# Attention and gated GELU block on one core: the pass over a unit's maxima set ahead of the V product, four bias additions and four closing additions dealt anew

## Chip, cores and metric

One core of one Trainium2 chip runs the whole program. The metric is the device time of one execution in microseconds. The time of a kernel is the median of several executions; a profile comes from one execution of its own, whose time is given beside its span.

## What is computed

The input x has 2048 tokens of 512 values. Its layer norm goes into two branches: attention with 32 heads of 16 values, and a dense block with a tanh-approximated GELU of 1376 hidden values, whose output goes through SiLU and gates the attention's output. x is added at the end.

```python
qkv = (xn @ wqkv).reshape(B, S, 3, H, Dh)           # xn = layernorm(x)
scores = einsum("bhqd,bhkd->bhqk", q, k) * Dh ** -0.5
s = einsum("bhqk,bhkd->bhqd", softmax(scores), v).reshape(B, S, D) @ wo
g = silu(gelu(xn @ w1 + b1) @ w2 + b2)
out = x + s * g
```

All matrices are f32. Most products are made of three: each factor is split into a high part (ScalarE's copy to the fp32r type) and a low part (the rest), and high x high, high x low and low x high are summed.

## The kernel before

**Work and its order.** The program's schedule is written out by hand; nothing is reordered. Each engine has one queue and works through it in order. The pools only give addresses. The program has three stages.

*Stage A* (to about 478 us): layer norm, the projections to Q, K and V, and the dense block. `down` multiplies hidden values by w2; the sums of four token tiles of 128 rows stand in four PSUM banks (`PA[c]`, one of `ps_v`, three of `ps_t`) and are taken out when a chunk `c` of 512 tokens is done (L649 to L661). For the first three chunks ScalarE copies the four tiles to SBUF (L656) and each becomes a `chore`: GpSimd adds the bias b2 (L666) and issues the store to `g_d` (L667); `half` calls one chore at a time. For the last chunk VectorE adds the bias straight from PSUM (L654), four times, and GpSimd issues the four stores (L661).

*The loop* (about 480 to 1545 us) works on 32 units: unit `u` is four heads and 512 queries. It has 513 steps, 16 for each unit. In a step, four score products with the keys in the partitions (`t_one`, letter T, L737) are each followed by an exponential on ScalarE (L739), and one V product (`pv_step`, letter V, L800) takes the exponentials of the step before. The exponential needs each query's largest score, which must be known ahead. So the loop also computes the scores of later units with the queries in the partitions (L190) and takes their maxima on VectorE (`s_max`, L195). A whole tile of these is letter S. Letters X and Y are two halves of one such tile, on the two row halves of TensorE, in one bank: Y must wait until X is finished, and this goes through a token, an instruction without work on GpSimd (in `s_op`, L227): it waits for X, and Y waits for it. The order of a step is a string, mostly `TSXTTSTYV`: three maxima a step. From step 50 on one step in 16 (that with two steps behind the end of a unit's V product) has `TSTTSTV`, two maxima.

**The end of a unit's maxima.** A unit has 64 maxima, and it reaches them in the middle of the loop's steps: 22 units (9 to 30) end in the part that matters here, the last (31) near step 491. `done` counts them, and at 64 the unit goes to `ended`. `s_end0` then takes one more pass over the unit's maxima on VectorE (`nm`, L250: 16 values for each partition out of 128), puts the split of `nm` into two parts on GpSimd into `put_off` (L253, L254, run behind the next token), has the queries of unit `u + 2` loaded, and puts the unit into `later` with a count (12 in stage A, 8 in the loop). Each V counts it down by 4; at zero `s_end1` transposes on VectorE (L269) and stores to `mh_d` through SP; `load_mh` reads it back for the score products.

Which maximum calls `s_end0` is decided in `s_max`, and there lies the first edit:

```python
done[u] += 1
if ended:
    s_end0(ended.pop())
if done[u] == 64:
    ended.append(u)
```

So `nm` stands one maximum behind the unit's last one: within the next step if that was a step's third, and at the same step's end if it was the second.

**Other lines used below.** At the last step of a unit's V product VectorE copies the bank `pv` to `os` (L807), which frees it for the next unit; `o_den` takes a reciprocal (L828), `o_div` a product (L837, GpSimd, for the last unit VectorE). Key loads of later heads are issued by GpSimd within the steps (L110).

*The end* (from 1545 us): the output projection (L81, L906) of the tokens that are left, the last four tiles (12 to 15) together. `w_gate` multiplies the product by the gate (L916), `w_add` adds x (L921) and stores through SP (L922). Tile 15 goes in two halves.

Of the kernel before, what the change touches and what calls it, by code (L numbers as in the profile page):

```python
# [16 lines left out]
P = 128  # L17
# [4 lines left out]
KT = D // P  # L22
NT = S // P
CH = 512
NCH = S // CH
# [24 lines left out]
def fused(ctx: ExitStack, tc: tile.TileContext, x, wqk, wv, wo, w1, b1, w2, b2, out):  # L50
    nc = tc.nc
# [92 lines left out]
    def load_qs(u, sides=range(2)):  # L144
        if u < NU:
            QS[u] = qzs[u % 2] if u < LEAD // 16 else qss[0][:, u % 2]
            q_rows(QS[u], u, sides)

    def ask_qs(u):
        errands[:0] = [(load_qs, u, (a,)) for a in range(2)]  # L150
# [13 lines left out]
    later, ended, errands, sent = [], [], [], set()  # L164

    def tick():
        for e in later:
            e[0] -= 1

    def flush():  # L170
        while later and later[0][0] <= 0:
            u = later.pop(0)[1]
            run_off()
            s_end1(u)

    def at_of(job):
        u, st, p = job
        return divmod(st, NCH) if u else divmod(st, NCH)[::-1]
# [13 lines left out]
    def s_max(ps, job, heads, parts):  # L192
        u, p = job[0], job[2]
        qi, ki = at_of(job)
        nc.vector.tensor_reduce(MX[u][:, 2 * p:2 * p + 2, qi, ki][:, heads, parts], ps.rearrange("p (n c) -> p n c", c=HC), axis=AX.X, op=OP.max)  # L195
        done[u] += 1
        if ended:
            s_end0(ended.pop())
        if done[u] == 64:
            ended.append(u)  # L200
        if done[NU - 1] == 64:
            s_end0(ended.pop())

    def s_whole(job, a):
        ps = s_tile()[0]
        s_mm(ps, job, a, 0, 0, CH)
        s_max(ps, job, a, slice(0, 2))
# [33 lines left out]
    def run_off():  # L241
        while put_off:
            put_off.pop(0)()

    def s_end0(u):
        later.append([12 if "seen" in prog else 8, u])
        nm = qring.tile([P, GH * NCH], F32, name="nm")
        hl = NM[u] = qring.tile([P, 2, GH * NCH], F32R, name="nmh")
        mx = MX.pop(u).rearrange("p a b c n -> p (a b) (c n)")
        nc.vector.tensor_reduce(nm, mx, axis=AX.X, op=OP.max, negate=True)  # L250

        def two():
            nc.gpsimd.tensor_copy(hl[:, 0], nm)  # L253
            nc.gpsimd.tensor_sub(hl[:, 1], nm, hl[:, 0].bitcast(F32))  # L254

        put_off.append(two)
        if "seen" in prog or u == NU - 1:
            run_off()
        del QS[u]
        if "seen" in prog:  # L260
            ask_qs(u + 2)
        else:
            load_qs(u + 2)

    prog = {}
# [14 lines left out]
    b2_sb = xp.tile([P, D], F32, name="b2_sb")  # L280
# [17 lines left out]
    for i in range(nu):  # L298
        pairs.append(ms[2 * i:2 * i + 2])
        if (i + 1) * len(qs) // nu > i * len(qs) // nu:  # L300
            g, c = qs[i * len(qs) // nu]
# [4 lines left out]
    for j in range(len(pairs)):  # L306
        for h in range(2):
# [9 lines left out]
            n = 2 if nd < len(parts) and parts[nd][2] and ready - nd > room else 1  # L317
            n = max(n, need - 2 * (left - 1))
            while nd < ready and n > 0:
                c, f, k = parts[nd]  # L320
# [25 lines left out]
    def w2_load(i):  # L346
        if i < len(ms):
            W2[ms[i][1:]] = w_new(w2[ms[i][2]], 2, "raw2")

    def w2_split(i):  # L350
        if i < len(ms):
            W2[ms[i][1:]] = w_split(W2[ms[i][1:]], "w2", W2B)
# [31 lines left out]
    with ExitStack() as s1:  # L384
# [14 lines left out]
        def load_x(t):  # L399
            xs[t] = w1k.tile([P, D], F32, name="xt", bufs=XB)  # L400
            eng = nc.scalar if t in (1, 3) else nc.sync
            eng.dma_start(xs[t], x[t * P:(t + 1) * P, :])
# [57 lines left out]
            W1[g] = w_new(wqk[:, g], 2, "raw1")  # L460
        for t in range(4, 6):
            load_x(t)
        for k in range(KT):
            nc.sync.dma_start(wv_r[:, k], wv[:, k])
        for t in range(6, XB):
            load_x(t)
# [112 lines left out]
    def mark(dve=False):  # L579
        if dve:  # L580
            i = nc.vector.tensor_copy(junk[:, 1:], ident_r[:1, :1].bitcast(F32)).ins
        else:
            i = nc.scalar.activation(junk[:, :1], ident_r[:1, :1].bitcast(F32), AF.Copy).ins  # L583
        tc.add_manual_dep(i, latest[0][1], SYNC, reason="row tile done")
        tokens.append((latest[0][0], i.name))

    def mark_early(n):
        if prog["seen"] < n:
            mark()
# [3 lines left out]
    def run(ops, hooks={}):  # L593
        for n, two in enumerate(zip(*ops)):
            prog["n"] += 1
            for a in range(2):
                fill(a)
                mm(a, *two[a])
            for h in hooks.get(n, []):
                h()  # L600
# [23 lines left out]
    PA, chores = {}, []  # L624

    def down(c, f, part):
        i = c * FT + f
        if f == 0 and part == 0:
            PA[c] = [ps_v.tile([P, D], F32, name="pv")] + [ps_t.tile([P, D], F32, name="pst") for t in range(3)]
        h, w = HS[c, f], W2[c, f]  # L630
        side = (part + i) % 2
        ops = [[], []]
        for a in range(2):
            for t in ((0, 1), (2, 3))[(a + side) % 2]:
                ts = slice(t * P, (t + 1) * P)
                for n, (x, y) in enumerate(((0, 0), (0, 1), (1, 0))):
                    ops[a].append(((c, t), PA[c][t], h[x][:, ts], w[y],
                                   f == 0 and part == 0 and n == 0, f == FT - 1 and part == 1 and n == 2))
        n = prog["pe"]
        if (c, f, part) == parts[-2]:  # L640
            run(ops, {2: [lambda: mark(True)], 5: [lambda: mark(True)]})
        else:
            run(ops, {3: [lambda: mark_early(n)]})
        if part == 0:
            w2_split(i + 1)
            w2_load(i + 3)
            return
        del HS[c, f], W2[c, f]
        if f == FT - 1:  # L649
            both = [wk.tile([P, 2, CH], F32R, name="gt") for i in range(2)]  # L650
            for n, t in enumerate((0, 2, 1, 3)):
                gt = both[n // 2][:, n % 2].bitcast(F32)
                if c == NCH - 1:
                    nc.vector.tensor_add(gt, PA[c][t], b2_sb)  # L654
                else:
                    nc.scalar.activation(gt, PA[c][t], AF.Copy)  # L656
                rs = slice(c * CH + t * P, c * CH + (t + 1) * P)
                if c < NCH - 1:
                    chores.append((gt, rs))
                else:  # L660
                    nc.gpsimd.dma_start(g_d[rs, :], gt)  # L661

    def chore():
        if chores:
            gt, rs = chores.pop(0)
            nc.gpsimd.tensor_add(gt, gt, b2_sb)  # L666
            nc.gpsimd.dma_start(g_d[rs, :], gt)  # L667

    def errand():
        if errands:  # L670
            f, *args = errands.pop(0)
            f(*args)
# [92 lines left out]
            load_mh(0)  # L765
    while errands:
        errand()
    del prog["seen"]
    s_ring.append(ps_x)
    qz.close()  # L770
# [108 lines left out]
    def cols(t):  # L879
        n = 2 if t == NT - 1 else 1  # L880
        return [slice(i * D // n, (i + 1) * D // n) for i in range(n)]
# [32 lines left out]
    def w_gate(t, i=0):  # L914
        gx, cs = GX[t], cols(t)[i]
        nc.vector.scalar_tensor_tensor(gx[:, 0, cs], PW[t][i][:, :cs.stop - cs.start], 0.5, gx[:, 0, cs],  # L916
                                       op0=OP.mult, op1=OP.mult)

    def w_add(t, eng, i=0):
        gx, cs = GX[t], cols(t)[i]  # L920
        eng.tensor_add(gx[:, 0, cs], gx[:, 0, cs], gx[:, 1, cs])  # L921
        nc.sync.dma_start(out[t * P:(t + 1) * P, cs], gx[:, 0, cs])  # L922

    def w_out(t, eng):
        w_gate(t)
        w_add(t, eng)
# [9 lines left out]
    def due(n):  # L936
        return min(4 * L, 4 * LEAD + max(0, 3 * n - 1 - max(0, (n - LIGHT) // 16)))

    for u in range(NU):
        g, c = divmod(u, NCH)  # L940
# [13 lines left out]
    T3 = range(NT - NCH, NT)  # L954
    late = range(NW, NT)
    for t in range(0, NW, 2):
        n = DONE + 2 * t
# [9 lines left out]
    for i, t in enumerate(late):  # L967
        n = L - 2 * len(late) - 1 + 2 * i
# [9 lines left out]
    for n in range(L + 1):  # L978
        ua, ka = divmod(n, 16)
        want = due(n) - due(n - 1)  # L980
        i = 0
        for op in ORDER[want] if n > 1 else ("TTTTV", "TVTSTST")[n]:
            if op in "SXY":
                s_op(op)
            elif op == "V":
                if n:
                    pv_step(*divmod(n - 1, 16))
                for _ in range(4):
                    tick()
                flush()  # L990
            else:
                if EARLY <= 4 * n + i < 4 * L:
                    t_one(ua, ka, i % 2, 1 - i // 2)
                for f, args in todo.get((n, i), []):
                    f(*args)
                i += 1
# [15 lines left out]
    for n, (t, i) in enumerate(ends):  # L1012
        w_mul(t, KS[-2:], (i,))
        w_gate(t, i)
        w_add(t, nc.vector if n else nc.gpsimd, i)


# [31 lines left out]
```

## Time and profile before

| what | value |
| --- | --- |
| median of 3 runs | 1568.05 us (1567.88 to 1568.91) |
| profiled execution | 1567.75 us |
| its span | 1566.0 us |
| granted TensorE clock | 1.00 |
| TensorE, VectorE, ScalarE, GpSimd busy | 99%, 89%, 79%, 24% of the span |
| from 490 to 1470 us: VectorE, ScalarE busy | 912.93 and 976.75 of 980 us |

In the profile PE is TensorE's products, PEld its loads of weights, DVE is VectorE, ACT ScalarE, POOL GpSimd and SP the queue of DMAs; a q behind a name is that engine's sequencer. A row of a timeline has the start and the duration in us, the engine, the line, the operation, out<-in with shapes, the count, and in brackets the idle time of the engine before it with what ended it. A row of the waits has the waiting engine, tile and line, who ended the wait, and total us, times and the longest. A row of the windows gives the stretch, then busy us and instructions of PE, PEld, DVE, ACT and POOL, the clock and the DMA share. Matmuls are pipelined, so TensorE's busy time holds waiting as well. Two instructions of one engine can overlap in their rows by some 0.1 us.

### The profile page before, as it was taken

Reading aid. Unit: us, or ns where it says so; the run is one execution under the profiler, and the core shown is the slowest. Engines: PE = TensorE matmul, PEld = TensorE weight load, DVE = VectorE, ACT = ScalarE, POOL = GpSimd, SP = SyncE. Lnnn points to the kernel's source line nnn. Section 1 sums busy time; section 2 is a strip of 40 time slices with the busy share of each in tenths; the row PEclk is TensorE's granted clock in tenths of the full one; section 3 lists DMA queues with packets and bytes.
Section 4 is the critical chain, followed back from the end, with each engine's and each line's share of the span. In section 5 each row is a group of like instructions: output and inputs, shape, how many; then the busy total and the mean of one; then the engine's idle time right before and its main releaser. Section 6 shows DMA issues by size and latency. Waiting matters only on the chain.

```text
span 1566.0 us, 32580 instructions
## 1 busy us (share of the span) xinstructions
PE 1555.4 (99%) x12254; PEld 955.0 (61%) x12254; DVE 1390.1 (89%) x2306; ACT 1244.4 (79%) x2487; POOL 375.4 (24%) x392
## 2 busy tenths in 40 slices
PE   8999999999999999999999999999999999999998
PEld 7899999999995444444444444444444444444455
DVE  7899999999998999999999999999999999999833
ACT  4333343434338999999999999999999999999994
POOL 4135574756752000000000100010110000000144
PEclk9999999999999999999999999999999999999999
DMA  6515443356435012311111311131141111110162
GB/s 217 159 47 139 116 156 108 112 148 152 140 89 117 21 42 43 60 30 30 43 29 28 65 30 43 43 73 36 36 73 30 33 29 30 43 30 22 45 209 104
DMA packets 79501, 117.38 MB, mean 75 GB/s; under 512 B 28876, under 2 KB 29132, under 8 KB 77968
## 3 DMA queue, kind: packets, MB, share of 16 engines
q1 hardware_dynamic: 75884, 102.36, 23.8%
q0 software_dynamic: 2976, 12.35, 4.4%
q8 instruction: 97, 1.59, 0.4%
q10 hardware_dynamic: 484, 0.60, 0.1%
q14 instruction: 60, 0.49, 0.1%
HBM read 84.81 MB, written 25.97 MB: 71 GB/s over the span
## 4 chain that ended last, share of the span: by engine, by line
PE 98%; DVE 1%; DMA 0%; issue 0%; POOL 0%; ACT 0%; DVEq 0%
PE pv L800 33%; PE pst L737 15%; PE ps L737 14%; PE ps L569 13%; PE ps L190 10%; PE pst L569 7%; PE pv L569 3%; PE ps L906 2%; PE ps L450 1%; PE ps L81 1%; PE pst L81 1%; DVE st L411 0%; DMA xt<-in_x 0%; PE pst L434 0%; DVE slot L76 0%; DVE xn L425 0%
## 5 line engine op out<-in xcount | busy, mean ns | idle before, releaser
L195 DVE TENSOR_REDUCE mx<-ps 128x2 f32<-128x512 f32 x2048 | 1297.3, 684 | 109.2 <-PE ps L190 29.1
L739 ACT ACTIVATE slot<-pst 128x512 f32<-128x512 f32 x1533 | 803.6, 604 | 2.9 <-PE ps L190 1.6
L800 PE MATMUL pv<-slot,vsb 128*17 128x512 f32 (+1 forms) x4096 | 539.2, 598 | 0.1
L190 PE MATMUL ps<-kt,slot 48*128 48x512 f32 x1350 | 382.7, 371 | 1.1 <-POOLq L227 1.1
L739 ACT ACTIVATE slot<-ps 128x512 f32<-128x512 f32 x515 | 307.9, 598 | 7.5 <-PE ps L737 4.7
L737 PE MATMUL pst<-qt,kt 50*128 50x512 f32 x1149 | 304.4, 405 | 0.0
L737 PEld LDWEIGHTS ps<-qt,kt 50*128 50x128 f32 x387 | 70.7, 183 | 323.8 <-ACT slot L739 322.9
L190 PEld LDWEIGHTS ps<-kt,slot 48*128 48x128 f32 x1350 | 223.1, 184 | 5.4 <-POOLq L227 1.4
L569 PE MATMUL ps<-slot,w1h 64*128 64x512 f32 x1104 | 222.3, 393 | 0.0
L737 PEld LDWEIGHTS pst<-qt,kt 50*128 50x128 f32 x1149 | 207.4, 184 | 21.3 <-DVE gt L654 1.2
L737 PE MATMUL ps<-qt,kt 50*128 50x512 f32 x387 | 190.9, 495 | 0.0
L190 PE MATMUL ps<-kt,qz 48*128 48x512 f32 x448 | 186.8, 417 | 0.0
L190 PE MATMUL ps<-slot,slot 48*128 48x512 f32 x584 | 168.5, 372 | 0.0
L569 PEld LDWEIGHTS ps<-slot,w1h 64*128 64x128 f32 x1104 | 156.0, 185 | 5.0 <-ACT junk L583 0.2
L569 PE MATMUL ps<-slot,w1l 64*128 64x512 f32 x552 | 145.3, 392 | 0.0
L370 POOL TENSOR_TENSOR hl<-hg,hh 128x512 fp32r<-128x512 f32 x76 | 96.9, 1297 | 134.6 <-ACT hh L369 94.4
L800 PEld LDWEIGHTS pv<-slot,vsb 128*17 128x17 f32 (+1 forms) x4096 | 68.8, 96 | 83.7 <-issue 31.6
L583 ACT ACTIVATE junk<-ident_r 1x1 f32<-1x1 f32 x94 | 18.4, 196 | 126.3 <-PE pst L569 118.2
L737 PE MATMUL pst<-qt,slot 50*128 50x512 f32 x384 | 99.6, 405 | 0.0
L190 PEld LDWEIGHTS ps<-slot,slot 48*128 48x128 f32 x584 | 97.1, 184 | 3.3 <-DVE mx L195 1.2
L837 POOL TENSOR_TENSOR slot<-slot,dn 64x512 f32<-64x512 f32 x16 | 20.5, 1281 | 312.4 <-PE pst L737 167.3
L190 PEld LDWEIGHTS ps<-kt,qz 48*128 48x128 f32 x448 | 82.0, 183 | 15.4 <-DVE mx L195 0.8
(153 smaller groups left out, 1764.2 us busy)
## 6 DMA issues: line engine op xcount, KB each, us to landing
raw<-in_w SPq DMA_DIRECT2D x88, 256.0 KB
qk_h<-hh SPq DMA_DIRECT2D x32, 256.0 KB
qk_l<-hl SPq DMA_DIRECT2D x32, 256.0 KB
qt<-qk_h SPq DMA_DIRECT2D x128, 64.0 KB
slot<-qk_h SPq DMA_DIRECT2D x92, 64.0 KB
g_d<-gt POOLq DMA_DIRECT2D x16, 256.0 KB, 3.0
qt<-qk_l SPq DMA_DIRECT2D x64, 64.0 KB
kt<-qk_h POOLq DMA_DIRECT2D x16, 256.0 KB, 6.4
```

The source lines that it names most:

```text
L81: nc.tensor.matmul(ps, lhs[a], rhs[b], start=first and n == 0, stop=last and n == 2)
L190: return nc.tensor.matmul(ps[:, c0:c0 + w], QS[u][r, p, qi * P:(qi + 1) * P], keys, start=True, stop=True).ins
L195: nc.vector.tensor_reduce(MX[u][:, 2 * p:2 * p + 2, qi, ki][:, heads, parts], ps.rearrange("p (n c) -> p n c", c=HC), axis=AX.X, op=OP.max)
L370: nc.gpsimd.tensor_sub(hl, raw, hh.bitcast(F32))
L450: nc.tensor.matmul(pq["q", g, c], W1[g][i][:, k * P:(k + 1) * P], (xh, xl)[j][c][:, k], start=n == 0 and k == 0, stop=n == 2 and k == KT - 1)
L569: i = nc.tensor.matmul(ps, lhs[r], rhs[r], start=first, stop=last).ins
L583: i = nc.scalar.activation(junk[:, :1], ident_r[:1, :1].bitcast(F32), AF.Copy).ins
L737: nc.tensor.matmul(ps, kts[KSET[g]][p][r, k * P:(k + 1) * P], QT[u][r, p, :], start=True, stop=True)
L739: nc.scalar.activation(PT[u, k][:, 2 * p + a, :], ps, AF.Exp, scale=SCALE)
L800: nc.tensor.matmul(PV[u][32 * j:32 * j + w, :], vsb[:, k, h:h + w], PT[u, k][:, j, :], start=(k == 0), stop=(k == NT - 1))
L837: eng.tensor_mul(ot[c][rs, g // 2], ot[c][rs, g // 2], DN.pop(u)[rs])
L906: op = nc.tensor.matmul(PW[b][0], OTS[b, k][i][r], (wo_h, wo_l)[j][r, k], start=part == 0 and n == 0, stop=part == 3 and n == 5).ins
```

## The change

Four edits:

1. The pass at a unit's end. In the loop `s_max` no longer calls `s_end0` (but for the last unit); a new `s_ended` does, which each letter V calls ahead of its product. In stage A everything stays. `nm` then always stands at the end of the step in which the unit's last maximum lies. The count of 8 starts at that V, so the transpose follows three maxima (two in a short step) behind `nm` and no longer up to five.
2. The last chunk's four tiles: two (n = 0, 2) as before, VectorE's addition and GpSimd's store. The other two (n = 1, 3) are copied by ScalarE and become chores, which are run right ahead of the loop: addition and store on GpSimd, twice.
3. The closing additions: tile 12's goes from GpSimd to VectorE, tile 14's from VectorE to GpSimd, with its store issued by ScalarE's queue instead of SP's.
4. The V weights come in three loads (1, 1 and 2 blocks) instead of four.

```diff
         done[u] += 1
-        if ended:
-            s_end0(ended.pop())
+        if "seen" in prog:
+            s_ended()
         if done[u] == 64:
             ended.append(u)
         if done[NU - 1] == 64:
+            s_end0(ended.pop())
+
+    def s_ended():
+        if ended:
             s_end0(ended.pop())
...
-        for k in range(KT):
+        for k in (slice(0, 1), slice(1, 2), slice(2, KT)):
             nc.sync.dma_start(wv_r[:, k], wv[:, k])
...
                 gt = both[n // 2][:, n % 2].bitcast(F32)
-                if c == NCH - 1:
-                    nc.vector.tensor_add(gt, PA[c][t], b2_sb)
-                else:
+                rs = slice(c * CH + t * P, c * CH + (t + 1) * P)
+                if c < NCH - 1 or n % 2:
                     nc.scalar.activation(gt, PA[c][t], AF.Copy)
-                rs = slice(c * CH + t * P, c * CH + (t + 1) * P)
-                if c < NCH - 1:
                     chores.append((gt, rs))
                 else:
+                    nc.vector.tensor_add(gt, PA[c][t], b2_sb)
                     nc.gpsimd.dma_start(g_d[rs, :], gt)
...
     while errands:
         errand()
+    while chores:
+        chore()
     del prog["seen"]
...
-    def w_add(t, eng, i=0):
+    def w_add(t, eng, i=0, queue=nc.sync):
         gx, cs = GX[t], cols(t)[i]
         eng.tensor_add(gx[:, 0, cs], gx[:, 0, cs], gx[:, 1, cs])
-        nc.sync.dma_start(out[t * P:(t + 1) * P, cs], gx[:, 0, cs])
+        queue.dma_start(out[t * P:(t + 1) * P, cs], gx[:, 0, cs])
...
             elif op == "V":
+                s_ended()
                 if n:
                     pv_step(*divmod(n - 1, 16))
...
-        w_add(t, nc.vector if n else nc.gpsimd, i)
+        if n == len(T3) - 2:
+            w_add(t, nc.gpsimd, i, nc.scalar)
+        else:
+            w_add(t, nc.vector, i)
```

## The prediction

> **What bounds the kernel now.** I read the page first (busy shares, then the chain that ended last), then the busy time of each engine in the attention loop, then who waits for whom, and last the timelines of single steps.
>
> ```profile
> span 1566.0 us, 32580 instructions
> PE 1555.4 (99%) x12254; PEld 955.0 (61%) x12254; DVE 1390.1 (89%) x2306; ACT 1244.4 (79%) x2487; POOL 375.4 (24%) x392
> 490.00:1470.00 980.00, 979.85 (x7636) 466.41 (x7636) 912.93 (x1517) 976.75 (x1923) 71.02 (x115) 1.00 0.19 40
> PEld ps L737 <- ACT slot L739: 431.7, 508, 0.9
> ```
>
> The chain runs through TensorE nearly throughout, but in the loop that names little: in 490 to 1470 us ScalarE is busy for 976.75 of 980 us, and 508 times, once a step, the loader of the weights waits for ScalarE's exponential (L739) to give a bank back. TensorE runs just ahead of ScalarE, four exponentials a step. So in the loop a change is worth what it takes from, or adds to, ScalarE's idle time, and that is 3.25 us in all: the most that anything done to VectorE there can bring.
>
> **Part 1: the pass over a unit's maxima (`nm`, L250).** Where ScalarE idles is seen in its first exponential of each step. From 484.00 to 506.30 us lie 11 steps, 2.03 us each; two steps are 4.06.
>
> ```profile
> 506.30 0.60 ACT L739 ACTIVATE slot<-ps 128x512 f32<-128x512 f32 x1
> 510.54 0.60 ACT L739 ACTIVATE slot<-ps 128x512 f32<-128x512 f32 x1
> 506.95 0.28 DVE L250 TENSOR_REDUCE nm<-mx 128x16 f32<-128x128 f32 x1
> 507.14 3.16 DVE L195 TENSOR_REDUCE mx<-ps 128x2 f32<-128x512 f32 x5
> ...
> 725.09 0.60 ACT L739 ACTIVATE slot<-ps 128x512 f32<-128x512 f32 x1
> 729.20 0.60 ACT L739 ACTIVATE slot<-ps 128x512 f32<-128x512 f32 x1
> 726.92 0.28 DVE L250 TENSOR_REDUCE nm<-mx 128x16 f32<-128x128 f32 x1
> ...
> 1438.50 0.60 ACT L739 ACTIVATE slot<-ps 128x512 f32<-128x512 f32 x1
> 1442.73 0.60 ACT L739 ACTIVATE slot<-ps 128x512 f32<-128x512 f32 x1
> ```
>
> Unit 9 ends at 506: `nm` stands behind the first of a step's three maxima, the pair of steps takes 4.24 us, 0.18 too long. Unit 30, the last that ends inside the loop's steady part, is alike (4.23). Unit 14 ends at 726: there the unit's last maximum was the second of its step, so `nm` came behind the third, just ahead of the V product, where VectorE has nothing to do: 4.11 us, 0.05 too long. A step's three maxima take 3 x 0.61 (507.14, 3.16 for five, the last one's tail included), which leaves 0.2 us free at the step's end; `nm` keeps VectorE for about that long (506.95 to 507.14). In the middle of a step it holds the second and third maximum, TensorE misses a bank and the V product starts late; at the end it fills the gap.
>
> The change puts every `nm` at that place. By the order of the changed program this alters 15 of the 22 unit ends of the loop (9, 11 to 13, 15 to 17, 20 to 22, 25 to 27, 29, 30); the other seven had it already. Eleven of the 15 become like unit 14. What that place costs, I read at the five ends that have it without other work beside them: 0.05, 0.03, 0.00 and 0.05 in four, and one outlier:
>
> ```profile
> 1124.66 0.60 ACT L739 ACTIVATE slot<-ps 128x512 f32<-128x512 f32 x1
> 1128.92 0.60 ACT L739 ACTIVATE slot<-ps 128x512 f32<-128x512 f32 x1
> ...
> 902.51 0.60 ACT L739 ACTIVATE slot<-ps 128x512 f32<-128x512 f32 x1
> 906.80 0.60 ACT L739 ACTIVATE slot<-ps 128x512 f32<-128x512 f32 x1 [0.20 <-PE ps L190]
> 904.54 0.68 DVE L807 COPY os<-pv 128x512 f32<-128x512 f32 x1
> ...
> 1391.70 0.60 ACT L739 ACTIVATE slot<-ps 128x512 f32<-128x512 f32 x1
> 1395.80 0.60 ACT L739 ACTIVATE slot<-ps 128x512 f32<-128x512 f32 x1
> ```
>
> Unit 23 (1124.66 to 1128.92) pays 0.20 at the good place. The mean of the five is 0.065, so 11 x (0.165 - 0.065) = 1.1 us gained. Unit 18 (902.51 to 906.80) shows the bad side: there `nm` stands directly ahead of `os` (L807), whose end frees the one bank of the V product, and the pair costs 0.23. The change makes unit 29 (now 4.10, 0.04) the same: 0.2 lost. Units 11 and 15 I put at 0.1 gained each, unit 21 at nothing. Sum of part 1: **-1.1 us**; bounds -3.25 (all of ScalarE's idle time) and +0.8 (rival 2). The transpose (L269) comes two maxima earlier too; its GpSimd work (L253, L254) stands where it stood, and at unit 14 three maxima are enough for it.
>
> **Part 2: two of the last four down outputs.** Before, VectorE adds the bias to all four and GpSimd issues four stores. Now ScalarE copies two, GpSimd adds the bias to them (two adds of L666's kind) and stores each.
>
> ```profile
> 477.26 1.58 ACT L739 ACTIVATE slot<-ps 128x512 f32<-128x512 f32 x3 [0.29 <-PE ps L737]
> 480.43 1.57 ACT L739 ACTIVATE slot<-pst 128x512 f32<-128x512 f32 x3 [1.60 <-PE ps L190]
> 484.00 0.60 ACT L739 ACTIVATE slot<-ps 128x512 f32<-128x512 f32 x1
> 478.69 1.87 DVE L654 TENSOR_TENSOR gt<-pst,b_sb 128x512 f32<-128x512 f32 x3
> 479.07 2.33 POOL L661 DMA_DIRECT2D g_d<-gt  x4 [1.02 <-DVE gt L654]
> 482.15 0.29 PE L190 MATMUL ps<-slot,slot 48*128 48x256 f32 x1
> 483.47 0.49 PE L737 MATMUL ps<-qt,kt 50*128 50x512 f32 x1
> ...
> 200.60 1.29 POOL L666 TENSOR_TENSOR gt<-gt,b_sb 128x512 f32<-128x512 f32 x1
> 202.19 0.56 POOL L667 DMA_DIRECT2D g_d<-gt  x1 [0.30 <-PE ps L190]
> 202.76 1.30 POOL L290 TENSOR_TENSOR w2l<-raw,w2h 128x512 fp32r<-128x512 f32 x1
> ```
>
> ScalarE's two copies cost nothing: it idles 1.60 us ahead of 480.43, and they need about 1.1 (two exponentials' time). VectorE's two saved adds (of 1.87 for three) bring nothing either: what starts ScalarE again is the score product that follows the first V product, and that V product waits only for the first output's add, which stays. The cost lies on GpSimd. In the loop, operation Y (`s_op`, a half-width score product) waits for GpSimd's token (L227), which comes behind all that GpSimd was given earlier, now including two adds and their stores. One add with its store takes 202.76 - 200.60 = 2.16 us. The first two stores end at about 480.2 (479.07 + 2 x 0.58); then 480.25 + 2 x 2.16 = 484.6 until the first token. The first Y ran at 482.15; it now runs at about 484.65, 2.5 us later. Behind it in TensorE's queue stand the V product and the next step's scores (483.47, 1.32 behind Y). ScalarE has seven exponentials in hand (the last ends at 484.0), then waits for that score: from 484.00 to 486.5. The loop runs at ScalarE's pace, so nothing catches up. That this wait is real, the trace of before shows near the end of the loop, where GpSimd is late with one token behind its work for `w_token`:
>
> ```profile
> 1480.98 0.39 PE L190 MATMUL ps<-kt,slot 48*128 48x256 f32 x1 [1.08 <-POOLq L227]
> ```
>
> Part 2: **+2.5 us**, bounds 0 (the token is in time after all) and 3.0 (the adds start behind slower copies). Also moved: the last of these stores lands some 3 us later, and SP's loads of the second unit's queries wait for that; they are wanted only a unit of 16 steps later, 33 us.
>
> **Part 3: the end.** The add for tile 12 goes from GpSimd to VectorE, the add for tile 14 from VectorE to GpSimd, and tile 14's store from SP to ScalarE's queue.
>
> ```profile
> 1557.87 1.30 POOL L921 TENSOR_TENSOR slot<-slot 128x512 f32<-128x512 f32 x1 [2.66 <-DVE slot L916]
> 1559.89 0.69 DVE L916 SCALAR_TENSOR_TENSOR slot<-ps,slot 128x512 f32<-128x512 f32 x1
> 1560.62 0.69 DVE L921 TENSOR_TENSOR slot<-slot 128x512 f32<-128x512 f32 x1
> 1561.68 0.42 DVE L921 TENSOR_TENSOR slot<-slot 128x256 f32<-128x256 f32 x1
> 1562.47 0.42 DVE L921 TENSOR_TENSOR slot<-slot 128x256 f32<-128x256 f32 x1
> ...
> 1552.21 1.29 POOL L921 TENSOR_TENSOR kt<-kt 128x512 f32<-128x512 f32 x1
> 1552.64 1.41 DVE L837 TENSOR_TENSOR ot<-ot,dn 64x512 f32<-64x512 f32 x1 [1.86 <-DMA dn<-den_d]
> ```
>
> Tile 12's add fits into VectorE's pause. Without the add of 0.69 at 1560.62 the last one would end at 1562.26 instead of 1562.89, 0.6 earlier. But at 1552.64 a VectorE product of two SBUF tiles took 1.41 us, twice the 0.69 of a like row, and ended 0.55 behind the end of the GpSimd add that ran beside it (1553.50). Tile 14's add now runs on GpSimd from about 1560.66 to 1561.96, and the first half of tile 15's add, due at 1561.05, meets it: if held the same way it ends at 1562.26, and the last add at about 1563.07, 0.2 later than before. The Trainium skill has this as a rule ("SBUF — State Buffer", "Who interferes with whom"): a VectorE instruction with two SBUF inputs and a GpSimd instruction that reads SBUF exclude each other, and the later one waits for the whole of the earlier. By that rule part 3 costs 0.2, without it it brings 0.6; the trace agrees with the rule. Part 3: **+0.2 us**, bounds -0.6 and +0.3.
>
> **Part 4: the V weights** come in three loads instead of four, the last of double size. Nothing waits for them: they are issued long before ScalarE takes them up (L503), which is only when its earlier work is done. 0, bounds +-0.2.
>
> **Sum.** -1.1 + 2.5 + 0.2 = +1.6 us. The profiled execution took 1567.75 us (span 1566.0, 1.75 around it), 0.3 under the median of the runs, 1568.05; the sum moves the one to 1569.35 and the median to **1569.65**. About 0.2%, 3.1 us, is what a measurement of this kernel can tell from no change.
>
> **Rivals.**
> 1. The late token is covered: GpSimd overlaps its adds with issuing stores, or Y has slack. For: only one token was late before, and its 1.08 us cannot be read apart in the steps' lengths there. Against: GpSimd's rows stand one behind the other everywhere. Then -1.1 + 0.2 = -0.9, 1567.15.
> 2. Slower: the pass is no cheaper at the new place. It gets 0.2 us of gap, and where the gap is filled already (a late maximum, `os`, a reciprocal) the V product slips; this decides if the new ends look like unit 23 or 18 (0.21) and not like unit 14. Then 15 ends turn from about 0.16 to 0.21: +0.8, and with parts 2 and 3 +3.5, 1571.55. For: two of the seven old ends with that order cost it. Against: four cost 0.05 or less.
> 3. A second hold on GpSimd: the key loads (L110) behind the tokens wait for the last store's landing, now near 488; they are reached at about 488.7. If it lands over 1.5 us later than I reckon, the next tokens slip too, by some 0.9: +2.5, 1570.55.
> 4. Everything good: no late token, all of ScalarE's 3.25 us gone, the end 0.6 shorter: -3.85, 1564.2.
>
> **How the numbers follow.** My forecast has 0.55 (1568.6 to 1570.7 by itself), rival 1 0.17, rival 2 0.14, rival 3 0.06, rival 4 0.08. Range 1566.7 to 1571.7: it takes in rivals 1 and 3 and half of rival 2, and leaves out rival 4. Faster by over 0.2% (below 1564.9) is nearly all of rival 4: 0.07. Slower (above 1571.2) is rival 2 and the tail of rival 3 with part of its sum: 0.16. The rest, 0.77, is within 0.2%.
>
> **What would show it.** In the changed profile: an idle time of TensorE with L231 (the token's new line) as releaser near 484.6, ScalarE idle about 2.5 us there; two adds and two stores on GpSimd from 480.2 to 484.6; pairs of steps of about 4.1 at units 9, 12 and 30, and 4.25 or more at unit 29; a VectorE add of 0.8 us or more in the end, beside GpSimd's. I am wrong if Y at the loop's start isn't late, if steps at unit ends stay at 4.23, or if the end is shorter by half a microsecond.

## The result and the profile after

| what | before | after |
| --- | --- | --- |
| median of 13 runs | 1567.91 us (1567.72 to 1568.91) | 1571.75 us (1570.05 to 1573.61) |
| ratio, 95% interval | | 1.0026 [1.0019, 1.0034] |
| profiled execution, its span | 1567.75 us, 1566.0 | 1571.6 us, 1569.7 |
| mean granted clock of the profiled execution | 1.00 | 0.998 |

The changed kernel is slower by 3.8 us, where +1.6 was forecast; its median lies 0.05 us above the range. The 13 runs fall into groups by their mean granted clock: one at 0.999 (1570.05), six at 0.998 (1571.37 to 1571.75), six at 0.997 (1572.51 to 1573.61). The groups are 1.3 to 1.6 us apart.

The first exponential of each step (L741 now), set against the same one before, tells where the time went. Until the loop's step 2 it comes 0.13 us earlier. At step 3 it is 2.57 us late (486.57 against 484.00) and at step 4 3.32. The rows are steps 3 and 4 after, then step 4 before:

```profile
486.57 0.60 ACT L741 ACTIVATE slot<-ps 128x512 f32<-128x512 f32 x1 [2.73 <-PE ps L190]
489.35 0.60 ACT L741 ACTIVATE slot<-ps 128x512 f32<-128x512 f32 x1 [0.71 <-PE ps L190]
...
486.02 0.60 ACT L739 ACTIVATE slot<-ps 128x512 f32<-128x512 f32 x1
```

Then it gains 0.09 to 0.16 at each of 12 unit ends, loses 0.36 at one, and reaches the loop's end 2.41 us late. The span ends 3.7 us late, so the end lost another 1.3.

**The loop's start.** The timeline of GpSimd and TensorE; the bracket has the idle time ahead of a row and what ended it:

```profile
480.21 1.30 POOL L668 TENSOR_TENSOR gt<-gt,b_sb 128x512 f32<-128x512 f32 x1
481.81 0.55 POOL L669 DMA_DIRECT2D g_d<-gt  x1 [0.30 <-POOL gt L668]
482.38 1.27 POOL L668 TENSOR_TENSOR gt<-gt,b_sb 128x512 f32<-128x512 f32 x1
483.95 0.55 POOL L669 DMA_DIRECT2D g_d<-gt  x1 [0.30 <-POOL gt L668]
484.00 0.38 PE L190 MATMUL ps<-slot,slot 48*128 48x256 f32 x1 [1.58 <-POOLq L231]
485.74 0.79 PE L739 MATMUL ps<-qt,kt 50*128 50x512 f32 x1
```

The first Y waits for the token as forecast, though to 484.00 instead of 484.65. It goes when the second store has its data (483.95), not when that store is done (484.50). But the score product behind it, 1.32 us behind Y before, is 1.74 behind it now and takes 0.79 instead of 0.49. The windows tell why; columns are the stretch, its length, the busy time of PE, PEld, DVE, ACT and POOL, then the granted clock, the DMA share and GB/s:

```profile
484.00:485.00 1.00, 1.00 (x9) 0.31 (x9) 0.58 (x1) 0.00 (x0) 0.49 (x1) 0.89 0.03 8
485.00:488.00 3.00, 3.00 (x16) 1.46 (x16) 1.38 (x3) 1.43 (x3) 0.00 (x0) 0.50 0.30 109
488.00:489.00 1.00, 1.00 (x10) 0.18 (x4) 0.71 (x2) 0.64 (x2) 0.00 (x0) 0.90 0.45 139
```

From 484.78 the clock is halved for about 3.41 us (0.22 + 3.00 + 0.20, from shares with two digits). Nothing of that was in the forecast.

**The unit ends.** ScalarE at unit 9 and unit 29, and VectorE at unit 29:

```profile
509.69 0.60 ACT L741 ACTIVATE slot<-ps 128x512 f32<-128x512 f32 x1
513.82 0.60 ACT L741 ACTIVATE slot<-ps 128x512 f32<-128x512 f32 x1
...
1393.93 0.60 ACT L741 ACTIVATE slot<-ps 128x512 f32<-128x512 f32 x1
1395.96 0.60 ACT L741 ACTIVATE slot<-ps 128x512 f32<-128x512 f32 x1
1398.37 0.60 ACT L741 ACTIVATE slot<-ps 128x512 f32<-128x512 f32 x1 [0.34 <-PE ps L190]
1395.89 0.29 DVE L254 TENSOR_REDUCE nm<-mx 128x16 f32<-128x128 f32 x1
1396.09 0.69 DVE L811 COPY os<-pv 128x512 f32<-128x512 f32 x1
490.00:1470.00 980.00, 979.54 (x7640) 468.68 (x7632) 913.91 (x1519) 977.60 (x1924) 71.89 (x117) 1.00 0.19 40
```

The pair of steps at unit 9 takes 4.13 us (4.24 before). At unit 29 `nm` now stands ahead of `os`, and the pair takes 4.44 (4.10). The last row is the loop's window: ScalarE is busy for 0.85 us more of the same 980.

**The end.** VectorE, then GpSimd; below them the groups of closing instructions (duration in ns as least, median and longest, then the first and the last start), after first, before second:

```profile
1563.47 1.15 DVE L925 TENSOR_TENSOR slot<-slot 128x256 f32<-128x256 f32 x1
1564.99 0.42 DVE L925 TENSOR_TENSOR slot<-slot 128x256 f32<-128x256 f32 x1
1563.07 1.27 POOL L925 TENSOR_TENSOR slot<-slot 128x512 f32<-128x512 f32 x1 [5.47 <-DVE slot L920]
L1053 POOLq DRAIN  x3: 46/107/5892, 1563.0 to 1569.5; - x3
L1053 SPq DRAIN  x3: 7/7/7, 1567.3 to 1569.2; - x3
```

```profile
L1045 POOLq DRAIN  x3: 46/107/5920, 1557.8 to 1565.7; - x3
L1045 SPq DRAIN  x3: 7/7/7, 1565.1 to 1565.4; - x3
```

VectorE's addition beside GpSimd's took 1.15 us instead of 0.42, and the last addition ends at 1565.41, 2.52 later than before: 0.11 more than the lag. But GpSimd's first DRAIN runs for 5.89 us from 1563.0, to 1568.9. Before, it ran from 1557.8 to 1563.75 and was over when SP began its own at 1565.1. Now SP is ready at 1567.3, and all wait for GpSimd.

### The profile page after: what moved, and what is told of

It reads as the page before. It is cut to its first block, busy times and chain, and to the rows that moved or that the text cites. A ratio compares the mean times of both kernels' runs of the same rounds, so it can differ in the third digit from the quotient of the medians.

```text
span 1569.7 us, 32578 instructions
## 1 busy us (share of the span) xinstructions
PE 1557.1 (99%) x12254; PEld 959.0 (61%) x12254; DVE 1390.3 (89%) x2304; ACT 1245.6 (79%) x2489; POOL 377.3 (24%) x394
## 4 chain that ended last, share of the span: by engine, by line
PE 98%; DVE 1%; DMA 0%; ACT 0%; POOL 0%; issue 0%; DVEq 0%; POOLq 0%
PE pv L804 32%; PE pst L739 15%; PE ps L739 14%; PE ps L573 13%; PE ps L190 10%; PE pst L573 8%; PE pv L573 3%; PE ps L910 1%; PE ps L454 1%; PE pst L81 1%; PE ps L81 1%; DVE st L415 0%; PE pst L438 0%; DMA xt<-in_x 0%; DVE slot L925 0%; DVE slot L920 0%
## 5 line engine op out<-in xcount | busy, mean ns | idle before, releaser
L741 ACT ACTIVATE slot<-pst 128x512 f32<-128x512 f32 x1533 | 804.0, 605 | 1.9 <-PE ps L190 0.6
L741 ACT ACTIVATE slot<-ps 128x512 f32<-128x512 f32 x515 | 307.5, 598 | 10.0 <-PE ps L190 4.5
```

The source lines that it names most:

```text
L741: nc.scalar.activation(PT[u, k][:, 2 * p + a, :], ps, AF.Exp, scale=SCALE)
```

## The experiments

### Three parts alone, and the theory of the end

The theory at this point: GpSimd's closing DRAIN ends some 4.6 us behind its last instruction, whatever that is. Each part is the change's own edit alone; the fourth kernel is the one before with only this added behind the last addition:

```diff
+    nc.gpsimd.tensor_copy(junk[:, 1:], GX[NT - 1][:1, 0, D - 1:])
```

> The kernel before with edit 1 alone (the pass over a unit's maxima ahead of the V product). Theory (each edit acts by itself): steps at 11 of the 15 changed unit ends lose 0.11 us each, unit 29 gains 0.36, so about 0.9 us less than before (1567.0). Rival (the pass costs the same wherever it stands, and the shrinking lag seen in the changed kernel comes from its late start being made good): no difference, 1567.9.

> The kernel before with edit 2 alone (two of the last four down outputs through ScalarE and GpSimd). Theory: TensorE waits some 1.6 us for GpSimd's token at the loop's start and then runs for 3.4 us at half the granted clock, together 3.3 us more than before, 1571.2, with the half clock in its record. Rival (the half clock is only how the hold is recorded, or comes from elsewhere in the changed kernel): the hold of 1.9 to 2.5 us alone, 1569.8 to 1570.4, clock 1.00 in the loop.

> The kernel before with edit 3 alone (closing additions and stores dealt anew). Theory: GpSimd's last addition ends some 2.6 us later than before, its closing drain takes 4.6 us from there and becomes the end of the program: 1.3 us more, 1569.2. Rival (only VectorE's held addition counts): 0.1 to 0.2 us more, 1568.1, and the span ends as long behind SP's last landing as before.

> The kernel before, with one copy of a single value on GpSimd behind the very last addition, and nothing else changed; no addition or store waits for it. Theory (GpSimd's closing drain takes about 4.6 us from its last instruction): that instruction ends near 1563.2, the drain near 1567.8 where all ended by 1565.2 before, so about 2.5 us more, 1570.4. Rival (what edit 3 costs at the end comes from its additions and stores): no difference, 1567.9.

Measured, with 1567.62 for the kernel before:

| kernel | median | lowest to highest | ratio, interval |
| --- | --- | --- | --- |
| part 1 | 1566.69 | 1566.48 to 1567.01 | 0.9993 [0.9985, 1.0002] |
| part 2 | 1570.94 | 1569.57 to 1572.67 | 1.0021 [1.0012, 1.0029] |
| part 3 | 1568.97 | 1568.65 to 1569.68 | 1.0009 [1.0000, 1.0018] |
| one-value copy at the end | 1570.13 | 1569.71 to 1571.93 | 1.0018 [1.0009, 1.0027] |

-0.9, +3.3 and +1.35 make +3.75, nearly the whole of what was lost (3.84). In the kernel with the copy only the end is touched. Its row, and its closing group:

```profile
1563.26 0.18 POOL L1016 COPY junk<-slot 1x1 f32<-1x1 f32 x1 [3.80 <-DVE slot L921]
L1046 POOLq DRAIN  x3: 46/107/4785, 1563.2 to 1568.6; - x3
L1046 SPq DRAIN  x3: 7/7/7, 1565.4 to 1568.3; - x3
```

A copy of 0.18 us cost 2.5 us: the DRAIN ended 4.59 us behind it (1563.24 + 4.79 against 1563.44). The gap is 4.58 with the additions of 1.3 us, before (1563.75 against 1559.17) and after (1568.92 against 1564.34). Part 3 alone is the same: its GpSimd addition ends at 1561.42, its DRAIN at 1566.00, SP was ready at 1564.8.

The profiled execution of part 2 alone was one without the half clock:

```profile
482.71 1.27 POOL L664 TENSOR_TENSOR gt<-gt,b_sb 128x512 f32<-128x512 f32 x1
484.28 0.55 POOL L665 DMA_DIRECT2D g_d<-gt  x1 [0.30 <-POOL gt L664]
484.33 0.38 PE L190 MATMUL ps<-slot,slot 48*128 48x256 f32 x1 [1.58 <-POOLq L227]
484.00:485.00 1.00, 0.67 (x5) 0.32 (x9) 0.25 (x1) 0.17 (x1) 0.55 (x1) 1.00 0.03 12
485.00:488.00 3.00, 3.00 (x28) 1.23 (x21) 2.25 (x4) 1.84 (x4) 0.00 (x0) 1.00 0.28 98
```

The same hold of 1.58 us, and the clock stays at 1.00. Here the first exponential of step 3 comes 1.96 us later against the kernel before than the one of step 2 did, and that is all that is lost. So the hold costs 2.0 us. What is above that in the median (3.3) goes with a lower clock: the four runs of part 2 below 1570.1 have a mean granted clock of 1.0, the seven above 1570.7 one of 0.997 to 0.999.

### What holds the token, and whether the idle array halves the clock

Two kernels add one or two subtractions on GpSimd ahead of the loop and nothing else (the results go nowhere):

```diff
+    for _ in range(2):
+        more = wk.tile([P, CH], F32R, name="hl", bufs=HB)
+        nc.gpsimd.tensor_sub(more, b2_sb, b2_sb)
```

Another has part 2 and, ahead of the first Y, 14 repeats of X's product of 48 rows, so that TensorE isn't idle while the token is held. The last has part 1 with the pass one place later:

```diff
             elif op == "V":
-                s_ended()
                 if n:
                     pv_step(*divmod(n - 1, 16))
+                s_ended()
```

> The kernel before, with one more subtraction of a 128x512 tile on GpSimd ahead of the loop, whose result nobody reads. Theory (all that GpSimd is given ahead of the first token moves the loop's start): GpSimd is free at 482.7 instead of 481.4, the first Y runs at 482.75 instead of 482.15, 0.6 us more, 1568.5, no half clock, since TensorE idles less than the 1.08 us that cost no clock in the kernel before. Rival (edit 2 costs through its copies and stores): no difference.

> The same with two subtractions. Theory: GpSimd is free at 483.95, close to edit 2's first token (483.93), the hold is 1.85 us and the half clock of 3.4 us comes with it: 3.3 us more, 1571.2. If the hold alone counts: 1.85 us more, 1569.8. Rival (copies and stores): no difference.

> Edit 2 alone, and ahead of the first Y its X is multiplied 14 times more into the same place, so that TensorE works while it would wait for GpSimd's token (the values stay the same). Theory (the wait by itself makes TensorE's clock fall to half): no half clock in the loop, the hold of about 1.9 us stays, 1569.8. Rival (the half clock has nothing to do with TensorE's idle time): 1571.2 as with edit 2 alone, or more by the extra products.

> The kernel before with edit 1, but the call stands behind the V product's instructions in the program and not ahead of them: where the V product of a unit ends in that step, the copy to os comes first and the pass second; all other unit ends are as in edit 1. Theory (units 18 and 29 cost some 0.2 to 0.35 us because the copy that frees the V product's bank waits for the pass): 0.4 us less than edit 1 alone, 1.3 us less than before, 1566.6. Rival (VectorE's sum of work at that place counts, not its order): as edit 1 alone, 1567.0.

| kernel | median | lowest to highest | ratio, interval |
| --- | --- | --- | --- |
| one subtraction | 1567.75 | 1567.65 to 1568.42 | 1.0001 [0.9992, 1.0010] |
| two subtractions | 1567.88 | 1567.67 to 1568.8 | 1.0001 [0.9992, 1.0010] |
| part 2, filled | 1572.46 | 1570.01 to 1573.04 | 1.0025 [1.0015, 1.0034] |
| part 1, behind the V product | 1566.46 | 1566.19 to 1567.89 | 0.9992 [0.9983, 1.0001] |

The two subtractions cost nothing, and their profile shows that the prediction's reason for the hold was wrong:

```profile
481.53 2.04 POOL L770 TENSOR_TENSOR hl<-b_sb 128x512 fp32r<-128x512 f32 x2
482.27 0.28 PE L190 MATMUL ps<-slot,slot 48*128 48x256 f32 x1
```

Y runs at 482.27, in the middle of GpSimd's work from 481.53 to 483.57. A token does not wait for the work that GpSimd has been given.

In the filled kernel TensorE was not idle, and the clock fell all the same:

```profile
483.15 2.34 PE L190 MATMUL ps<-slot,slot 48*128 48x256 f32 x15
486.00:489.00 3.00, 3.00 (x20) 1.46 (x16) 1.20 (x3) 1.15 (x3) 0.00 (x0) 0.50 0.28 102
```

(The last of the 15 is Y.) Three of the 10 runs took 1570.0 to 1570.3, seven 1571.7 to 1573.0. In these runs a filler of 48 of the array's 128 rows kept the clock no better than idleness.

With the pass behind the V product `os` goes first at unit 29, and the loss there is gone: the pair of steps takes 4.10 us.

```profile
1390.32 0.60 ACT L743 ACTIVATE slot<-ps 128x512 f32<-128x512 f32 x1
1394.42 0.60 ACT L743 ACTIVATE slot<-ps 128x512 f32<-128x512 f32 x1
1392.15 0.68 DVE L811 COPY os<-pv 128x512 f32<-128x512 f32 x1
1392.75 0.28 DVE L254 TENSOR_REDUCE nm<-mx 128x16 f32<-128x128 f32 x1
490.00:1470.00 980.00, 980.00 (x7648) 468.87 (x7644) 914.33 (x1520) 978.14 (x1926) 70.80 (x115) 1.00 0.19 40
```

ScalarE is busy for 1.39 us more of the loop's 980 than before, against 0.85 in the changed kernel; the span is 1564.5, 1.5 shorter than before.

### The two stores through SyncE

If it is a store's wait for its addition that holds the token, the additions may stay on GpSimd and only the stores have to go:

```diff
-    def chore():
+    def chore(queue=nc.gpsimd):
...
-            nc.gpsimd.dma_start(g_d[rs, :], gt)
+            queue.dma_start(g_d[rs, :], gt)
...
     while chores:
-        chore()
+        chore(nc.sync)
```

With it ran part 2 with a filler of 26 products of the whole array (`ident_r` with itself, 128 rows by 128 columns), part 4 alone, and a version of the two pieces that seemed to gain or to be free: the pass behind the V product and part 2 with its stores on SyncE; the end and the V weights as before.

> Part 2 alone (alone it took 1570.94), but the two last stores that wait for GpSimd's additions are issued by SyncE instead of GpSimd; the additions stay on GpSimd. Theory (the token of the first Y is a sequencer instruction and is held only behind the store's own wait for its addition): the token comes in time, by 482.2, no idle of TensorE before the first Y, no half clock behind it, and 1567.2 to 1568.0, as before. Rival (the token comes behind the additions themselves, as the prediction had it): the first Y still at 484 or later and 1569.8 to 1571.5. A third way (SyncE's wait for the additions holds back its own later loads): the token in time, but a wait for a query load or for a running maximum some us later, up to +1.

> Part 2 alone, with 26 products of 128 rows by 128 columns (about 1.5 us) put ahead of the first Y, where TensorE stood idle, so that the whole array works while the token is held. The other filler had 48 rows and did not do away with the half clock. If the idle array is what halves the clock: nearly all runs at 1569.6 to 1570.2, none at 1571.4 or above, granted clock 1.0 from 482 to 490. If the half clock comes from something else (a load of the array by its window, whatever is in it): the same spread as with part 2 alone, 1569.6 to 1572.7, with about half of the runs above 1571. The fill itself may add up to 0.7 where it is longer than the hold.

> The late pass over the maxima set behind the V product's step instead of ahead of it (alone -1.3), with part 2 in the form whose two stores go through SyncE (expected 0 by the theory). Theory: 1566.2 to 1566.7, faster than before and than the changed kernel by about 1.3 and 5. Rival (the additions hold the token): 1568.5 to 1570.

> The fourth part of the change alone: the loads of the V weights, one for each of the blocks, become three. The prediction takes 0: 1567.6 to 1568.0, ratio within 0.0005. Rival: fewer starts on SyncE's queue let the later loads of x begin sooner by some 0.3 us for each one saved, worth up to -0.5 if the start of the kernel waits for them; or the one large load lands later than the first blocks need it, up to +0.5.

| kernel | median | lowest to highest | ratio, interval |
| --- | --- | --- | --- |
| before | 1567.94 | 1567.37 to 1568.94 | |
| part 2, stores on SyncE | 1567.7 | 1567.4 to 1568.29 | 0.9998 [0.9989, 1.0007] |
| part 2, long full filler | 1572.04 | 1571.11 to 1574.91 | 1.0029 [1.0017, 1.0040] |
| late pass and stores on SyncE | 1566.28 | 1565.83 to 1566.89 | 0.9989 [0.9980, 0.9998] |
| part 4 | 1567.39 | 1567.13 to 1567.79 | 0.9996 [0.9988, 1.0005] |

GpSimd and TensorE with the stores on SyncE:

```profile
480.24 2.53 POOL L664 TENSOR_TENSOR gt<-gt,b_sb 128x512 f32<-128x512 f32 x2
482.04 0.30 PE L190 MATMUL ps<-slot,slot 48*128 48x256 f32 x1
```

Both additions run on GpSimd until 482.77, Y runs at 482.04 with no idle time ahead of it, and all of part 2's 3.3 us are gone. So the token was held behind the stores, not behind the additions. Whether any store given ahead of it would hold it, or only one that still waits for its addition, these two kernels don't tell apart. The combined version beats both kernels: 1.7 us under the kernel before, with the whole interval below 1, and 5.5 under the changed one.

The full filler failed as an experiment: 26 products took 3.1 us, not 1.5, and held Y to 486.75 themselves. Four of six runs lie at 1571.1 to 1572.4, two at 1574.2 and 1574.9.

### The half clock once more, and part 4

Twelve products of the whole array in place of 26; part 2 with all four outputs through ScalarE and GpSimd (the condition `if c < NCH - 1 or n % 2` becomes true for all), so that four stores stand ahead of the token; and the combined version with part 4 added.

> Part 2 with 12 products of 128 rows by 128 columns ahead of the first Y (0.11 us each, 1.3 us in all, as the longer filler's rows show), instead of 26. If the idle array halves the clock: the first Y at about 485.0, most runs within 1569.8 to 1570.8 and at most 2 of 11 above 1571.4. If the idle array is not the cause: half of the runs or more above 1571.4, as with part 2 alone (median 1570.94, 7 of 11 above 1570.7).

> Part 2 taken further: all four last outputs go through ScalarE's copy and GpSimd's addition, so that four stores that wait for their additions stand ahead of the token, 1.85 to 1.95 us apart as with two (the second token came 1.9 after the first store). Theory of the held sequencer: the first Y about 3.8 us later than with two such stores, at 488, and TensorE idle for 5 us or more. If idleness halves the clock, all runs have a half-clock stretch (mean clock 0.999 or lower, none at 1.0), one or two of them, and the median is 1575 to 1576.5. If not: 1573.4 to 1574.2 in several runs, with the same mixture as with part 2 alone. Rival (VectorE, relieved of two more additions, starts its maxima earlier and gives part back): 1 less in either case.

> The late pass behind the V product's step, part 2 with its two stores on SyncE, and part 4's loads of the V weights in three starts. Without part 4 this was 1566.28. If part 4 is worth the 0.2 to 0.5 that its own run hinted at: 1565.8 to 1566.1. If it is worth nothing: 1566.2 to 1566.4.

| kernel | median | lowest to highest | ratio, interval |
| --- | --- | --- | --- |
| before | 1567.91 | 1567.52 to 1569.38 | |
| part 2, short full filler | 1570.19 | 1569.66 to 1573.29 | 1.0020 [1.0011, 1.0029] |
| part 2 with four outputs | 1575.77 | 1574.67 to 1576.36 | 1.0050 [1.0038, 1.0063] |
| combined, with part 4 | 1566.35 | 1566.19 to 1567.21 | 0.9991 [0.9982, 1.0000] |

Filled hold, from the profile of the short filler, then the long hold with four outputs:

```profile
482.87 1.56 PE L237 MATMUL ps<-ident_r 128*128 128x128 f32 x12
484.56 0.38 PE L190 MATMUL ps<-slot,slot 48*128 48x256 f32 x1
```

```profile
487.89 0.55 POOL L665 DMA_DIRECT2D g_d<-gt  x1 [0.30 <-POOL gt L664]
487.94 0.58 PE L190 MATMUL ps<-slot,slot 48*128 48x256 f32 x1 [4.42 <-POOLq L227]
488.00:491.00 3.00, 3.00 (x13) 0.99 (x15) 0.69 (x1) 0.00 (x0) 0.43 (x1) 0.50 0.23 87
491.00:494.00 3.00, 3.00 (x18) 0.93 (x14) 1.98 (x3) 2.06 (x4) 0.00 (x0) 0.50 0.42 126
```

With four stores Y goes again just when the last one has its data, 3.6 us later than with two, after 4.42 us of idleness. There the clock is halved for 6.83 us, two such stretches, from 487.19 on, while TensorE still idles; and all five runs have a mean clock of 0.998 or less. With the short full filler six of 11 runs took 1569.7 to 1570.2, two 1571.4 to 1571.5 and three 1572.6 to 1573.3; with part 2 alone it was four of 11 up to 1570.1, four of 1570.8 to 1571.2 and three above. Five against seven of 11 above 1570.7 is no difference that so few runs can show, and five are there though the array was at work. Part 4 adds nothing to the combined version.

The traces also show when the clock can change. In each of them its changes lie a whole number of 3.413 us apart, up to the last one, near the end. In the changed kernel they come at 6.92, 484.78, 488.20 and 1566.81 (140, 1 and 316 such lengths), in the kernel before at 5.07 and 1564.96 (457). The first comes 4.2 to 7.2 us behind the start, another time in every execution, so the hold meets these lengths at another place each time. These rows are the length in which the hold, or its filler, lies for the most part: in the changed kernel, with part 2 alone, with the filler of 48 rows and with the short full filler:

```profile
481.37:484.78 3.41, 1.83 (x14) 0.86 (x12) 1.89 (x4) 2.46 (x6) 2.52 (x4) 1.00 0.35 130
482.91:486.33 3.42, 2.00 (x16) 0.93 (x16) 1.15 (x3) 1.43 (x4) 1.62 (x2) 1.00 0.42 159
482.30:485.71 3.41, 3.28 (x24) 2.59 (x26) 1.67 (x4) 2.41 (x5) 2.49 (x4) 1.00 0.33 121
482.41:485.82 3.41, 3.28 (x24) 1.91 (x22) 1.69 (x3) 1.94 (x4) 2.29 (x3) 1.00 0.33 126
```

The clock was halved behind the first (TensorE busy for 1.83 us) and the third (3.28), and not behind the second (2.00) and the fourth (3.28). So TensorE's busy time in such a length doesn't decide by itself.

## Why the prediction was right or wrong

**Part 1, forecast -1.1: right.** Alone it brought 0.9. The interval of that still holds 1, but the changed kernel's trace shows the gain at the steps that were named: 12 unit ends gain 0.09 to 0.16 each (11 with 0.10 were reckoned, and two with 0.1), unit 29 loses 0.36 for `os` where 0.2 was reckoned. Rival 2 (a pass no cheaper at its new place) did not come.

**Part 2, forecast +2.5: the right place, a wrong reason, and a term left out.** The wait, its releaser and the stretch it falls into were as predicted. The step that failed is "comes behind all that GpSimd was given earlier": 2 us of subtractions hold no token, and neither do the two additions without their stores. The token is held by a store on the same queue that waits for an addition. That lets it go when the second store has its data, so the hold was about 2.0 us and not 2.5. The row that the prediction took as a proof of its reason (Y at 1480.98, after 1.08 us of idleness) has another reading. These are GpSimd and ScalarE before it, in the kernel before:

```profile
1479.94 2.51 POOL L868 TENSOR_TENSOR ol<-slot,oh 128x512 fp32r<-128x512 f32 x2 [23.13 <-PE pst L737]
1480.21 0.66 ACT L867 ACTIVATE oh<-slot 128x512 fp32r<-128x512 f32 x1
```

Y goes in the middle of GpSimd's two subtractions (1479.94 to 1482.45), 0.11 us behind the end of the ScalarE copy (1480.87) that the second one waits for. That fits a token held by an instruction ahead of it that still waits, there a subtraction; no run changes this place alone. The Trainium skill ("Perfetto Trace Analysis", "DMA Instruction — SWDGE (GPSIMD)") has the sequencer free for the next instruction as soon as the store is pushed into a wait queue. By that rule the token would have been in time; the runs say otherwise here (Y at 484.00, 0.35 us behind the second addition's end), and the measurement decides.

The term left out is the clock. In the profiled execution a stretch of 3.41 us at half speed follows the hold, and 12 of the 13 runs have a mean clock of 0.998 or less, as it has. It took the loss there from about 2 to 3.45 us: the hold's 1.98 (Y came 1.85 later, and up to there the kernel had been 0.13 ahead), 0.72 more up to the exponential of step 3 (the score product came 0.42 later behind Y and took 0.30 longer), and 0.75 in the next step. The six runs at 0.997 are another 1.3 us longer; none of them has a trace. The Trainium skill ("TensorE: Matmul & The Clock Gate", "What's actually happening") gives a free-running window of 3413 ns after which an idle array is gated to half; the length agrees with the 3.41 us, and the changes of the clock 3.413 us apart agree with a free-running window. With four stores a whole window (483.78 to 487.20) was idle, as that rule has it; in the changed kernel none was (1.83 us of work from 481.37 to 484.78), and the clock fell as well. What the runs don't settle is how little work sets it off. By the mean clocks, 4.42 us of idleness did so in all five runs and 1.58 us in some; a filler of 48 of the 128 rows did not prevent it, and a filler of the whole array, by the times, did not in five of 11. The first products behind the hold (ScalarE and VectorE have run dry then, as their busy times 0.00 and 0.58 in the window of 484 to 485 show) may count as much as the idle time itself; this wasn't tried.

**Part 3, forecast +0.2: right on the path that was looked at, and the end lay on another.** VectorE's addition ended late beside GpSimd's, as the rule that the prediction cites has it (1.15 us, 0.8 or more forecast), and the last store was 0.11 late. The step that failed is the one not taken: GpSimd's last instruction was moved 2.8 us closer to the end (from 1557.87 to 1563.07, less the lag of 2.4), and its closing DRAIN lies 4.58 us behind that. In the profile of before that DRAIN was covered by 1.4 us (1563.75 against 1565.1); the forecast did not ask what covered it. The term is +1.3, and the copy of one value, with no addition moved, shows it by itself.

**Part 4, forecast 0: right.** -0.5 alone, with an interval that holds 1, nothing beside the other edits (1566.35 against 1566.28).

The misses make the 2.1 us between forecast and result: +1.3 for the half clock (an estimate: 3.3 in the median of part 2 less the hold's 2.0), +1.1 for the DRAIN (1.3 less 0.2), +0.2 for part 1, and -0.5 for the shorter hold (2.0 less 2.5). Rival 3 did not occur: no key load held a later token.

## What to carry to other kernels

A late instruction on an engine that was long done is not free even when its result comes in time: look at what the engine still has to do behind its last work, and by how much the other queues' ends cover that. Before work is put ahead of a signal on a queue, ask which instruction ahead of it waits, not how much work there is: two additions cost nothing, their two stores 2 us. And where a hold of a microsecond and a half is added to TensorE, reckon with a second loss behind it in the clock; here it was 1.5 us in the changed kernel's trace, beside a hold of 2.0.

## What was not expected of the hardware

- GpSimd's closing DRAIN ended 4.58 or 4.59 us behind its last instruction's end in four kernels, whether that was an addition of 1.3 us or a copy of 0.18.
- GpSimd's tokens overtake its running work (Y at 482.27 during work from 481.53 to 483.57), but not a store that waits.
- Idleness of 1.58 us ahead of the first Y went with 3.41 us at half clock in the changed kernel's trace and with none in that of part 2 alone; 4.42 us went with 6.83 us. The clock's changes lay whole multiples of 3.413 us apart.
